# Squared-ReLU attention and a gated MLP on one core: loading and turning q and k of batches 2 to 7 in another way

## The chip, the core and the metric

The kernel runs on one core of a Trainium2 chip. The metric is the time of one execution on the device in microseconds (us). The core has five engines that each work through their own instructions in order: TensorE (PE), VectorE (DVE), ScalarE (ACT), GpSimd (POOL) and SyncE (SP, which only issues DMAs here). PEld is the loading of weights into TensorE, which overlaps its matmuls. DMAs run on 16 DMA engines; SP, ACT and POOL issue them.

## What is computed

```python
# q, k, v: (8 batches, 12 heads, 448 positions, 64), float32
scores = scale * np.matmul(q, k.transpose(0, 1, 3, 2))
attn = np.maximum(scores, 0.0) ** 2 / S
x = (attn @ v).transpose(0, 2, 1, 3).reshape(B * S, H * D)     # (3584, 768)
h = x @ w_in                                                   # w_in  (768, 2048)
g = h * (1.0 / (1.0 + np.exp(-1.702 * h)))
out = g @ w_out                                                # w_out (2048, 768)
```

All products are made in fp16 with sums in float32; the scale and 1/S are applied later, in the gelu (L201) and on the way out.

## The kernel before, in words

**Units.** A batch has three units of four heads, so there are 24 units (unit 0 to 23; batch b has units 3b to 3b+2). For each unit the kernel needs q and k turned, with the head dimension on the partitions: `qT` and `kT`, 7 blocks of 128 columns each. A unit's scores are made block by block (`scores`, L147, 64x64 parts of the array, two PSUM banks a block); `relu` (L158 on DVE, L160 on ACT) brings them to SBUF as `at`, `square` (L85, L166) squares them, and `attn_v` (L178) multiplies by v into two banks; `xt_evac` copies these into `xb`, the transposed input of the MLP.

**q and k before.** Units 0 to 5 come in one way, the others in another. Unit 0 is loaded in float32 by SP (`load`, L96) and cast; units 1 to 5 are loaded by GpSimd with a cast to fp16 on the way (`load_cast`, L101). These six are turned by TensorE (`trans_pe`, L128), 14 matmuls with the identity a tile, each giving 64 columns of weights to one half of the array, and copied from PSUM (`trans_evac`, L76 or L80). Units 6 to 23 are loaded in float32 by SP (`load`) into `qst` and `kst`, one buffer each, cast by POOL, ACT or DVE (`cast`), and turned by a DMA transpose that SP issues (`trans_dma`, L116). The fp16 tiles have two buffers for q and two for k. v is always loaded by GpSimd with a cast (four buffers).

**The MLP.** A batch's first product is made with 16 blocks of w_in. Batch 0 makes it plainly (`m1`, L214, tile `ht`); from batch 1 on a seven-product scheme is used (`unit_product`, L194, tile `hx`), with sums prepared by DVE and with snapshots, additions and gelus by ACT and DVE. Each gelu leaves a float32 tile `gf` (five buffers, used in turn); `widen` (L204) scales it into the fp16 `ring`, on POOL or DVE, and that frees the gf tile. The second product (`pair_product`, L194, tile `ox`) takes two row blocks at a time by the same scheme; the results go to `osb` and out by SP (`store`).

**The order of the work** is written out by hand, as one list of short words that the loop `do` runs through under a manual schedule. Every engine gets its instructions in the order of the words, and so do the DMA queues of SP and POOL. The words that matter here: `Lq6`, `Lk6` are float32 loads by SP of unit 6, `jq4`, `jk4` casting loads by POOL, `V4` the same of v; `Q6:a` and `K6` casts, `Rq6` and `Rk6` DMA transposes; `tq4@4` the turning by TensorE into PSUM bank 4, `eq4` its copy to SBUF; `s4.6` scores of block 6 of unit 4, `r4.6.1` a relu, `x4.6` a square, `a4` the product with v, `e4.0` its copy; `jwa0`, `jwb0` the two halves of a quarter of w_in, `jo0.1` a quarter of w_out; `f0.4.1` a third of the plain product of block 4 of batch 0, `g0.4` its gelu, `v0.4` its widening; `u1.2.0` one of the seven products. `:a`, `:d` and `:p` choose ACT, DVE or POOL, and `@` the PSUM banks.

A wait of one instruction holds up whatever stands behind it on its engine. GpSimd's DMAs of both kinds of work stand in one queue with its widenings and casts.

Of the kernel before, what the change touches and what calls it, by code (L numbers as in the profile page):

```python
# [8 lines left out]
F32 = mybir.dt.float32  # L9
F16 = mybir.dt.float16  # L10
AF = mybir.ActivationFunctionType
ALU = mybir.AluOpType
# [3 lines left out]
def kernel(  # L16
# [31 lines left out]
    for name, bufs in (("cst", 1), ("kst", 1), ("qst", 1), ("k16", 2), ("q16", 2), ("v16", 4),  # L48
                       ("kT", 3), ("qT", 3), ("at", 15), ("xb", 2),
                       ("T1", 1), ("T2", 1), ("T4", 1), ("gf", 5),  # L50
                       ("as0", 1), ("as1", 1), ("osb", 3)):
        pool(name, bufs)
# [10 lines left out]
    gate = const("gate", [1, 64])  # L63
# [30 lines left out]
    def load(n, u):  # L94
        x = new(f"{n}st", [128, 2, S], F32)
        nc.sync.dma_start(out=x, in_=quad(n, u))  # L96
        units[u][n + "st"] = x
# [6 lines left out]
    def cast(n, e, u):  # L104
        x = units[u].pop(n + "st")
        if u == 0:
            c = new(f"{n}16", [128, 2, S], F16)
            copy(e, c, x)
        else:
            c = new(f"{n}16", [128, J, 2, D], F16)  # L110
            copy(e, c.rearrange("p j a d -> p a j d"), x.rearrange("p a (j d) -> p a j d", d=D))
        units[u][n + "16"] = c

    def trans_dma(n, u):
        t = new(f"{n}T", [128, J, 128], F16)
        nc.sync.dma_start_transpose(  # L116
            out=t[:, :, :], in_=units[u].pop(n + "16").rearrange("p j a d -> p (j a d)"))
        units[u][n + "T"] = t
# [4 lines left out]
    def trans_pe(n, p, u):  # L123
        ps = bank(p, "tr", F16)
        x = units[u].pop(n + "16")
        for j in range(J):
            for a in range(2):
                nc.tensor.matmul(  # L128
                    out=ps[64 * a:64 * a + 64, j * 128:(j + 1) * 128],
                    lhsT=x[:, a, 64 * j:64 * j + 64], rhs=ident[:, :], is_transpose=True)  # L130
        units[u][n + "ps"] = ps
# [176 lines left out]
    def store_part(e, p, m, h, i):  # L308
# [3 lines left out]
            NOUT + NOUT // 2 * (h - 2), NOUT + NOUT // 2 * (h - 1))  # L312
# [32 lines left out]
    def pair_product(e, p, m, n, h=None):  # L345
        c = (0, 1, 0, 1, 0, 0, 1)[n] if h is None else 2 + h
        if n < 2 or (n == 3 and h is not None):
            op[m, c] = bank(p, "ox")
# [4 lines left out]
        mm(op[m, c][:, k], lambda f: a[:, f, :], lambda f: w[:, f, k], HF, n in (0, 1, 3))  # L353

    def pair_snap(e, p, m, n):
        i, c = {0: (0, lo), 2: (0, hi), 4: (1, hi)}[n]
        copy(e, out_tile(m + i)[:, c], op[m, 0][:, 0:NOUT], 1.0 / SC)

    def pair_last(e, p, m, n, h=None):
        i, c = {1: (0, lo), 3: (1, hi), 5: (1, lo), 6: (0, hi)}[n]  # L360
        o = out_tile(m + i)[:, c][:, quarter(h)]
        if n == 5:
            copy(e, o, op[m, 0][:, 0:NOUT], 1.0 / SC)
        else:
            x = op[m, 1 if h is None else 2 + h][:, quarter(h)]
            nc.vector.scalar_tensor_tensor(out=o, in0=x, scalar=1.0 / SC, in1=o,  # L366
                                           op0=ALU.mult, op1=ALU.add)
# [13 lines left out]
    def sp_gate(e, p, i):  # L381
        nc.sync.dma_start(out=gate[0:1, :], in_=win[i][127:128, 0, 0:64])

    with tc.manual_schedule():
# [4 lines left out]
               "G": sp_gate,  # L389
# [3 lines left out]
        for n in "kq":  # L393
# [3 lines left out]
            two["R" + n] = lambda e, p, u, n=n: trans_dma(n, u)  # L397
# [22 lines left out]
        def zeros(e, p, n):  # L420
# [8 lines left out]
            "z9@0 z1 z1 jq1 z1 z1 jk1 V1 I Lq0 Lk0 z1 z1 z1 Q0:d tq0@1 eq0:a K0:d tk0@2 tq1@3 ek0 "  # L429
            "eq1 s0.5@4.5 jq2 r0.5.1:d r0.5.0 s0.1@6.7 jk2 s0.2@0.1 r0.2.1 r0.1.1:d jq3 s0.0@2.3 "  # L430
            "s0.3@5.4 r0.1.0 r0.2.0:d r0.3.1 r0.3.0:d s0.4@1.7 tk1@6 ek1 s1.6@0.4 s1.4@5.6 jk3 x0.2 "
            "r0.0.0 V0 r0.4.1 r0.0.1 x0.0 r0.4.0 r1.6.0 s0.6@2.7 x0.3 jwa0 s1.0@3.1 r1.6.1 r1.0.1 "
            "tq2@0 x0.5 eq2 s1.5@4.1 r1.4.1 r1.5.0:d s1.3@0.6 jwb0 r1.4.0 r1.5.1 V2 s1.1@4.5 x1.6 "
            "tk2@1 jq4 r1.3.1 jwb2 x1.4 r0.6.1 ek2 r1.1.1 x0.4 jk4 r0.6.0 jwa2 r1.1.0 r1.0.0 tq3@6 "
            "s2.3@7.1 eq3 x0.1 r1.3.0 r2.3.0 s1.2@5.2 r1.2.1 jwa1 x1.1 jwb1 x0.6 tk3@4 r2.3.1 ek3 "
            "jq5 V3 a0@3.6 r1.2.0 jk5 x1.0 jwb3 x1.2 x1.3:a s2.4@0.7 e0.1:a e0.0:a r2.4.0 s3.3@2.1 "
            "x1.5 r3.3.0:d r3.3.1 r2.4.1:d a1@4.5 e1.0:a V4 e1.1:a s2.2@6.3 r2.2.1:d jwa3 s2.5@0.2 "
            "V5 r2.2.0 x2.3 f0.2.0@1 r2.5.0 jo1.0 s2.0@7.4 r2.0.1 s2.1@5.3 r2.1.1 r2.0.0:d r2.5.1 "
            "f0.2.1 jo0.0 x2.2 f0.3.0@6 r2.1.0:d f0.3.1 x2.0 s2.6@0.4 r2.6.1 r2.6.0 s3.1@3.7 r3.1.0 "
            "s3.0@2.5 r3.1.1:d jo1.1 tq4@4 f0.1.0@0 jo0.1 r3.0.0:d eq4 x2.4 x2.6 x2.1:a f0.1.1 "  # L440
            "s3.2@3.7 x2.5:a r3.2.0 a2@2.4 tk4@3 r3.2.1:d r3.0.1 e2.0:a s3.6@7.5 e2.1 ek4 f0.3.2 "
            "r3.6.0:d x3.2 r3.6.1 f0.2.2 g0.3 g0.2 f0.1.2 g0.1 s3.5@2.4 s3.4@3.7 r3.4.0 r3.4.1 "
            "r3.5.0:d s4.4@5.6 r4.4.0:d r4.4.1 v0.2 f0.0.0@1 x3.3 f0.0.1 f0.0.2 f0.8.0@0 g0.0 "
            "s4.5@3.7 r3.5.1:d S0.1 r4.5.0 s4.6@2.5 r4.6.0:d s4.3@6.1 v0.1 f0.8.1 r4.3.0 f0.8.2 "
            "x3.6 r4.6.1 x3.5 x3.0 g0.8 v0.3 s4.2@4.3 r4.2.1 S1.1 s4.1@2.6 r4.2.0 f0.4.0@5 f0.4.1 "
            "f0.5.0@0 f0.4.2 r4.1.0 f0.5.1 x4.6:a x4.2:a G3 v0.8 f0.6.0@3 f0.6.1 r4.3.1:d r4.5.1:d "
            "x3.1 S2.1 f0.6.2 f0.5.2 x4.4 x3.4 f0.7.0@4 g0.6 tq5@2 eq5 S1.2 tk5@1 r4.1.1 g0.4 Lq6 "
            "Lk6 S2.2 ek5:a g0.5 a3@7.3 e3.1:a v0.5 s4.0@2.6 s5.2@5.1 r5.2.1 r4.0.0:d f0.11.0@0 "
            "r4.0.1:d f0.11.1 r5.2.0 f0.11.2 e3.0:a x4.0 x4.5 s5.0@3.1 g0.11 s5.4@2.6 x4.3:a r5.0.1 "
            "s5.5@5.7 f0.7.1 r5.5.1 f0.9.0@0 f0.9.1 f0.9.2 r5.0.0:d f0.7.2 r5.5.0:d s5.3@1.7 r5.4.1 "  # L450
            "x4.1 v0.6 g0.7 a4@3.5 S3.1 s5.1@6.4 r5.3.1 r5.4.0 S2.4 v0.11 v0.7 x5.0:a Q6 r5.3.0:d "
            "s5.6@7.2 S1.3 e4.0 f0.10.0@1 g0.9 S3.2 f0.10.1 v0.9:d r5.6.1 r5.1.1:d u1.2.0@3 S0.3 "
            "f0.15.0@0 x5.3:a f0.14.0@2 r5.1.0 x5.1 f0.15.1 r5.6.0:d v0.4 f0.15.2 f0.14.1 x5.2:a "
            "v0.0 g0.15 f0.10.2 x5.4 T1.1 f0.14.2 u1.3.0@4 g0.10 x5.6:a f0.13.0@6 x5.5 K6 Lk7 "
            "a5@7.0 f0.13.1 S1.4 e4.1:a S3.4 S0.2 S2.3 Lq8 f0.13.2 v0.10:d e5.0:a v0.15:d e5.1:a "
            "Rq6 T1.2 u1.0.0@1 u1.1.0@5 u1.1.1@7 S0.4 t1.0.0 Rk6 g0.14 t1.1.0 T1.3 v0.14:d b1.1.1 "
            "u1.0.2 g0.13 u1.0.1@0 u1.1.2 t1.0.2 u1.0.4 v0.13 b1.0.1 g1.1.1 v1.1.1 W1.1 g1.0.1 "
            "v1.0.1 S3.3 t1.1.2 f0.12.0@2 u1.0.3 t1.0.4 u1.1.4 t1.2.0 T1.4 b1.0.3 u1.1.3 t1.1.4 "
            "u1.3.1@6 g1.0.3 u1.0.6 K7 W2.1 b1.1.3 b1.0.6 u1.0.5 Lk8 f0.12.1 W0.1 v1.0.3 u1.1.6 "
            "u1.2.1@0 g1.0.6 W3.1 b1.1.6 g1.1.3 u1.1.5 b1.2.1 v1.0.6 g1.0.5 u1.2.2 t1.3.0 v1.1.3 "  # L460
            "u1.2.3 g1.2.1 v1.0.5:d v1.2.1 W3.2 t1.2.2 b1.3.1 f0.12.2 W0.2 W0.3 g1.1.6 u1.2.4 g0.12 "
            "p0.0@7 v0.12 t1.2.4 W1.3 Q8:a b1.2.3 v1.1.6 Lq7 u1.2.5 A0.1@0 g1.2.3 W3.3 u1.3.2 Rq8 "
            "A0.2@1 g1.2.5 W2.2 h0.0 u1.2.6 b1.2.6 g1.3.1 v1.3.1 u1.3.3 g1.1.5 W2.4 W1.2 t1.3.2 "
            "p0.1@1 V6 v1.1.5 Rk7 s6.0@2.3 r6.0.0:d A0.3 r6.0.1 v1.2.5 s6.1@0.5 r6.1.0 l0.1 u1.3.4 "
            "t1.3.4 r6.1.1 p0.2 A0.4 x6.0:a s6.2@2.3 r6.2.1 h0.2:d r6.2.0:d s6.4@0.5 r6.4.1 p0.3 "
            "W2.3 b1.3.3 Q7:a W0.4 s6.3@3.2 r6.3.1 x6.1 p0.4 W1.4 K8:p r6.4.0 r6.3.0 W3.4 h0.4 "
            "x6.3:a Rq7 Lk9 l0.3 Lq9 x6.4 u1.3.5 s6.5@5.2 s6.6@0.3 r6.6.1 g1.3.5 r6.6.0 x6.2 u1.3.6 "
            "r6.5.1:d p0.5 r6.5.0 b1.3.6 g1.2.6 s7.0@3.4 l0.5 v1.2.6 r7.0.0:d x6.5 r7.0.1 x7.0 "
            "s7.2@0.2 r7.2.1 s7.4@5.6 r7.4.1 p0.6 s7.1@7.3 s7.6@4.2 r7.4.0 V8 V7 v1.3.5 r7.1.0:d "
            "Rk8 x7.4 x6.6:a r7.1.1 a6@6.5 r7.6.0 s7.3@7.3 K9:p l0.6 Q9 r7.6.1 e6.0:a r7.3.0:d "  # L470
            "r7.3.1 s7.5@4.1 r7.5.0 Lk11 e6.1 p2.0@2 x7.6 r7.2.0 Rk9 s8.5@6.7 s8.4@3.4 x7.1 "
            "s8.2@5.0 r7.5.1 r8.5.1 r8.2.1 Rq9 p2.1@1 A2.1@1 s8.1@7.0 r8.2.0:d r8.4.1 r8.4.0 x7.2 "
            "x7.3 r8.5.0 r8.1.0:d K11:p s8.3@5.4 r8.1.1 x7.5:a r8.3.0 Rk11 r8.3.1:d x8.1:a a7@3.6 "
            "s8.0@7.0 s8.6@5.4 r8.6.0 r8.6.1 A2.2@0 h2.0:d r8.0.1:d Lq10 e7.1:a p2.2 o1 r8.0.0:d "
# [150 lines left out]
```

## Time and profile before

| | us |
|---|---|
| median of 3 runs | 362.71 (362.51 to 363.19) |
| profiled execution | 363.36 |
| its span | 361.6 |
| TensorE idle in the span | 9.8 |
| instructions in the span | 9118 |
| casting loads by GpSimd, q, k, v | 34, 224 KB each as written |
| float32 loads by SP, q and k | 38, 448 KB each |
| DMA transposes by SP | 36 |

The page of a profile shows busy times by engine, the same in 40 slices of the span, the DMA queues, the chain of waits that ended last, and groups of instructions by line and form. Other views of the same trace give stretches of time, the instructions of an engine in order, and who waited for whom. The granted TensorE clock is full throughout. A busy TensorE is not one at its peak: the ends of matmuls are modelled, so distances are read from start to start.

### The profile page before, as it was taken

How to read it: one execution, taken by the hardware profiler on the slowest of the kernel's cores; microseconds unless marked ns; L12 is line 12 of the kernel's file. 1: busy time of each engine (PE TensorE's matmuls, PEld its weight loads, DVE VectorE, ACT ScalarE, POOL GpSimd, SP SyncE). 2: the span in 40 equal slices, each digit the busy share in tenths (PEclk: the TensorE clock that was granted, in tenths of full speed). 3: DMA queues.
4: the chain of work that ended last, by engine and by line, in shares of the span. 5: the costliest groups of instructions: out<-in, count | busy, mean ns of one | idle time of the engine just before them, and what ended most of it. 6: DMA issues, size and time to landing. Idle time of an engine off the chain costs nothing.

```text
span 361.6 us, 9118 instructions
## 1 busy us (share of the span) xinstructions
PE 351.8 (97%) x3600; PEld 240.6 (67%) x3600; DVE 313.2 (87%) x578; ACT 286.0 (79%) x551; POOL 116.9 (32%) x169
## 2 busy tenths in 40 slices
PE   8799999999999999999999999999999999999995
PEld 4444458854579655896568865698579756778663
DVE  3999999999998899899988898989998898674844
ACT  3999898999988998789997799868987898427410
POOL 5735731435135424242244343254121310102000
PEclk9999999999999999999999999999999999999999
DMA  8999999679889999868699625980381101130314
GB/s 178 159 195 205 217 234 240 126 122 229 189 224 268 210 164 182 204 121 199 145 195 172 198 33 86 210 200 0 68 175 46 44 2 45 45 87 2 87 45 133
DMA packets 65388, 51.39 MB, mean 142 GB/s; under 512 B 35776, under 2 KB 62016, under 8 KB 65344
## 3 DMA queue, kind: packets, MB, share of 16 engines
q1 hardware_dynamic: 48336, 36.32, 43.0%
q0 software_dynamic: 16608, 14.09, 26.7%
q8 instruction: 28, 0.46, 0.5%
q10 hardware_dynamic: 400, 0.39, 0.3%
q14 instruction: 16, 0.13, 0.1%
HBM read 45.61 MB, written 11.01 MB: 157 GB/s over the span
## 4 chain that ended last, share of the span: by engine, by line
PE 85%; DMA 6%; DVE 4%; ACT 2%; POOL 2%; issue 1%; POOLq 0%
PE ox L194 34%; PE hx L194 32%; PE sc L147 8%; PE av L178 7%; DMA k<-in_k_dram 3%; DMA q<-in_q_dram 3%; PE ht L214 3%; PE zp L424 1%; DVE at L85 1%; DVE at L158 1%; POOL ring L204 1%; ACT at L160 1%; ACT gf L201 1%; PE tr L128 0%; DVE asum L85 0%
## 5 line engine op out<-in xcount | busy, mean ns | idle before, releaser
L160 ACT ACTIVATE at<-sc 128x448 f16<-128x448 f32 x214 | 104.9, 582 | 7.3 <-PE sc L147 7.2
L204 POOL TENSOR_SCALAR ring<-gf 128x448 f16<-128x448 f32 x94 | 58.0, 617 | 156.1 <-ACT gf L201 152.7
L194 PE MATMUL ox<-wout,ring 128*128 128x384 f16 (+1 forms) x456 | 80.3, 324 | 0.1
L194 PEld LDWEIGHTS <-ring 128*128 128x128 f16 x568 | 53.7, 98 | 35.9 <-issue 6.1
L158 DVE TENSOR_SCALAR at<-sc 128x448 f16<-128x448 f32 x122 | 72.2, 616 | 3.6 <-PE sc L147 2.7
L194 PEld LDWEIGHTS <-win 128*128 128x128 f16 x672 | 64.0, 98 | 6.6 <-issue 3.0
L85 DVE TENSOR_TENSOR at<-at 128x896 f16<-128x896 f16 x102 | 63.1, 644 | 0.3
L166 ACT ACTIVATE at<-at 128x896 f16<-128x896 f16 x66 | 62.7, 969 | 0.8 <-DVE at L158 0.5
L85 DVE TENSOR_TENSOR gf<-hx,gf 128x448 f32<-128x448 f32 x84 | 51.1, 620 | 10.8 <-PE hx L194 4.9
L201 ACT ACTIVATE gf<-gf 128x448 f32<-128x448 f32 x84 | 46.8, 573 | 15.1 <-DVE gf L85 14.9
L194 PE MATMUL hx<-xb,win 128*128 128x224 f16 x504 | 58.0, 259 | 0.0
L147 PE MATMUL sc<-qT,kT 64*64 64x448 f16 x672 | 49.7, 358 | 2.0 <-DVE kT L80 1.4
L194 PEld LDWEIGHTS <-winS 128*128 128x128 f16 x504 | 48.2, 98 | 2.7 <-issue 1.1
L76 ACT ACTIVATE gf<-hx 128x448 f32<-128x448 f32 x59 | 31.4, 542 | 13.2 <-PE hx L194 9.5
L194 PE MATMUL ox<-wT,asum 128*128 128x384 f16 (+1 forms) x232 | 41.0, 321 | 0.7 <-DVE osb L366 0.5
L194 PE MATMUL hx<-T,winS 128*128 128x224 f16 x336 | 39.7, 259 | 0.0
L178 PE MATMUL av<-at,v 64*64 64x448 f16 x672 | 37.1, 350 | 1.2 <-ACT at L160 0.7
L147 PEld LDWEIGHTS <-kT 64*64 64x64 f16 x672 | 18.0, 105 | 25.9 <-issue 18.8
L194 PEld LDWEIGHTS <-asum 128*128 128x128 f16 x232 | 21.4, 98 | 16.8 <-issue 4.4
L366 DVE SCALAR_TENSOR_TENSOR osb<-ox,osb 128x384 f32<-128x384 f32 (+1 forms) x44 | 23.3, 533 | 8.9 <-PE ox L194 6.9
L178 PEld LDWEIGHTS <-v 64*64 64x64 f16 x672 | 19.8, 106 | 14.0 <-issue 2.8
L80 POOL CAST q<-qst 128x896 f16<-128x896 f32 x13 | 13.4, 1028 | 39.6 <-DMA qT<-q 14.5
(57 smaller groups left out, 363.3 us busy)
## 6 DMA issues: line engine op xcount, KB each, us to landing
out_dram<-osb SPq DMA_DIRECT2D x52, 192.0 KB, 3.4
qst<-in_q_dram SPq DMA_DIRECT2D x19, 448.0 KB, 4.9
kst<-in_k_dram SPq DMA_DIRECT2D x19, 448.0 KB, 4.4
v<-in_v_dram POOLq DMA_DIRECT2D x24, 224.0 KB, 5.7
win<-in_moe_w_in_dram POOLq DMA_DIRECT2D x8, 384.0 KB, 12.3
wout<-in_moe_w_out_dram POOLq DMA_DIRECT2D x4, 768.0 KB, 20.6
q<-in_q_dram POOLq DMA_DIRECT2D x5, 224.0 KB, 5.3
k<-in_k_dram POOLq DMA_DIRECT2D x5, 224.0 KB, 5.9
```

What stands on the lines that cost most here:

```text
L76: nc.scalar.activation(out=o, in_=i, func=AF.Copy)
L80: eng[e].tensor_copy(out=o, in_=i)
L85: eng[e].tensor_tensor(out=o, in0=x, in1=y, op=op)
L147: nc.tensor.matmul(out=sc[a][c, 0:S], lhsT=st["kT"][r, j, c], rhs=st["qT"][r, :, c], start=True, stop=True)
L158: nc.vector.tensor_scalar(out=o, in0=i, scalar1=0.0, scalar2=None, op0=ALU.max)
L160: nc.scalar.activation(out=o, in_=i, func=AF.Relu)
L166: nc.scalar.activation(out=at, in_=at, func=AF.Square)
L178: nc.tensor.matmul(out=av[s][64 * a:64 * a + 64, 0:S], lhsT=v16[r, a, 64 * j:64 * j + 64], rhs=at[r, a, :], start=(j == 0), stop=(j == J - 1))
L194: nc.tensor.matmul(out=o, lhsT=lhs(i), rhs=rhs(i), start=start and i == 0, stop=i == n - 1, skip_group_check=True)
L201: nc.scalar.activation(out=o, in_=i, func=AF.Gelu_apprx_sigmoid, scale=1.0 / SC)
L204: eng[e].tensor_scalar(out=o, in0=i, scalar1=SC, scalar2=1.0, op0=ALU.mult, op1=ALU.mult)
L366: nc.vector.scalar_tensor_tensor(out=o, in0=x, scalar=1.0 / SC, in1=o, op0=ALU.mult, op1=ALU.add)
```

## The change

All units but unit 0 are now loaded by GpSimd's casting DMA and turned by TensorE in 64-column tiles; there are no DMA transposes, no `qst` and `kst`, and no casts but unit 0's two. q and k in fp16 have four buffers each. Unit 0 is loaded in float32 by SP into the space of `ring`, which is not yet in use, and turned by 7 matmuls of 128 columns a tile. The last row pairs may be split in other quarters. The whole list of words is in a new order, and the choices of engine and bank are new.

The counts of words, before and after: casting loads of q and k 10 and 46; float32 loads 38 and 2; turnings by TensorE 12 and 48; copies of turned tiles 10 on DVE and 2 on ACT, then 31 and 17; relus 214 on ACT and 122 on DVE, then 230 and 106; widenings 94 on POOL and 34 on DVE, then 85 and 43. The numbers of score, v, w_in and w_out products are the same.

```diff
-    for name, bufs in (("cst", 1), ("kst", 1), ("qst", 1), ("k16", 2), ("q16", 2), ("v16", 4),
+    for name, bufs in (("cst", 1), ("k16", 4), ("q16", 4), ("v16", 4),
...
-        x = new(f"{n}st", [128, 2, S], F32)
-        nc.sync.dma_start(out=x, in_=quad(n, u))
-        units[u][n + "st"] = x
+        o = "kq".index(n) * 4 * S
+        x = ring.rearrange("p f c -> p (f c)")[:, o:o + 4 * S].bitcast(F32)
+        units[u][n + "st"] = x.rearrange("p (a c) -> p a c", a=2)
+        nc.sync.dma_start(out=units[u][n + "st"], in_=quad(n, u))
...
-    def trans_dma(n, u):
-        t = new(f"{n}T", [128, J, 128], F16)
-        nc.sync.dma_start_transpose(
-            out=t[:, :, :], in_=units[u].pop(n + "16").rearrange("p j a d -> p (j a d)"))
-        units[u][n + "T"] = t
...
         for j in range(J):
+            if len(x.shape) == 2:
+                nc.tensor.matmul(out=ps[:, j * 128:(j + 1) * 128],
+                                 lhsT=x[:, j * 128:(j + 1) * 128], rhs=ident[:, :],
+                                 is_transpose=True)
+                continue
             for a in range(2):
                 nc.tensor.matmul(
...
-        if n < 2 or (n == 3 and h is not None):
+        if n < 2 or h is not None:
...
-    def sp_gate(e, p, i):
-        nc.sync.dma_start(out=gate[0:1, :], in_=win[i][127:128, 0, 0:64])
...
-        "z9@0 z1 z1 jq1 z1 z1 jk1 V1 I Lq0 Lk0 z1 z1 z1 Q0:d tq0@1 eq0:a K0:d tk0@2 tq1@3 ek0 "
-        "eq1 s0.5@4.5 jq2 r0.5.1:d r0.5.0 s0.1@6.7 jk2 s0.2@0.1 r0.2.1 r0.1.1:d jq3 s0.0@2.3 "
...
+            "Lq0 Lk0 z9@0 jq1 jk1 jq2 jk2 jq3 z1 Q0:d z1 z1 I z1 z1 z1 z1 V0 tq0@1 K0:d eq0:a jwa0 "
+            "tk0@2 jk3 ek0 tq1@3 eq1 V1 s0.4@4.5 s0.2@6.7 s0.0@0.1 r0.4.0 r0.4.1:d s0.6@2.3 jq4 "
...
+            "jq8 r3.0.1 tq4@1 r3.2.0:d r3.2.1 tk4@4 jo0.1 x2.5:a x2.3 x2.6 a2@3.6 jk7 r3.0.0 ek4 "
+            "eq4:a jq7 f0.2.0@5 e2.1 f0.2.1 e2.0:a V6 x3.4 s4.5@4.1 s3.6@6.3 r4.5.0:d r4.5.1 f0.3.2 "
+            "r3.6.0 f0.2.2 r3.6.1:d f0.0.2 g0.3 x3.0 f0.1.2 g0.2 s4.3@4.1 g0.0 s4.1@6.3 v0.2 "
+            "s3.5@0.5 r4.3.0:d r4.1.0 f0.8.0@7 v0.0 r4.1.1:d r3.5.1 f0.8.1 f0.10.0@4 g0.1 jk8 x4.1 "
+            "f0.8.2 x3.6:a S0.1 f0.10.1 f0.10.2 x3.2 r3.5.0 s4.0@6.3 v0.3:d r4.3.1 s3.1@5.2 "
+            "r4.0.0:d tk5@0 r3.1.1 tq5@1 g0.10 ek5 f0.6.0@6 r3.1.0 S2.1 f0.6.1 g0.8 x3.3 f0.6.2 "
+            "r4.0.1 f0.4.0@2 v0.8 eq5 x3.1:a f0.4.1 x3.5 jk9 f0.4.2 x4.0 s4.2@4.0 g0.4 s4.6@5.7 jq9 "
+            "a3@3.1 S2.2 g0.6 v0.4 r4.2.0:d r4.2.1 r4.6.1 v0.10 s5.5@2.6 s5.0@4.0 e3.1 r5.5.1 v0.6 "
+            "f0.7.0@7 r5.0.1:d r5.5.0 f0.7.1 v0.1 f0.7.2 e3.0:a r5.0.0:d r4.6.0 s4.4@1.6 V8 S1.1 "
+            "s5.4@0.2 s5.1@3.4 r4.4.0 x4.2 f0.12.0@5 r4.4.1 f0.15.0@1 x4.6 g0.7 f0.12.1 x4.4 r5.4.0 "
```

## The prediction

> **What bounds the kernel now.** I read the engine table first, then the chain of waits, then the windows by stage, then the waits.
>
> ```profile
> PE 351.8 (97%) x3600; PEld 240.6 (67%) x3600; DVE 313.2 (87%) x578; ACT 286.0 (79%) x551; POOL 116.9 (32%) x169
> DMA  8999999679889999868699625980381101130314
> ```
>
> TensorE is busy 97% of the span. The DMA engines are at 9 tenths in nearly every slice (9.04 us each) of the first 63 us. The windows show where TensorE is really the limit (columns: stretch, length, busy us and count of PE, PEld, DVE, ACT, POOL, clock, DMA share, GB/s):
>
> ```profile
> 0.00:54.00 54.00, 49.53 (x590) 25.95 (x590) 46.95 (x87) 45.54 (x91) 30.23 (x45) 1.00 1.15 198
> 54.00:306.00 252.00, 251.12 (x2599) 177.29 (x2599) 233.40 (x429) 221.13 (x423) 82.37 (x117) 1.00 0.71 147
> ```
>
> From 54 us, where the last product of attention and v of batch 1 (unit 5) starts, to 306 us, TensorE idles 0.9 us: what is added there lengthens the run. Before 54 us it gets through only 590 matmuls, and there the chain of waits (start, length, what) does not run through it:
>
> ```profile
> 14.55 9.83 DMA q<-in_q_dram
> ...
> 24.92 11.79 DMA k<-in_k_dram
> ...
> 37.00 0.87 POOL wout L376
> ...
> 37.95 2.26 POOL ring L204
> ...
> 40.23 0.54 ACT gf L201
> ```
>
> This is read as follows. GpSimd's DMAs complete on eight semaphores in turn, so each waits until the eighth one before it has landed: k of unit 5, the 20th, is issued at 24.92 when q of unit 4, the 12th, has landed; the 28th (w_out, 37.00) goes when the 20th has. Only then does GpSimd reach its first widening (L204), which frees one of the five gf tiles for which ScalarE's gelu (L201) waits; the waits give 1.76 us for that. GpSimd's DMA queue is thus one link from the path in the start.
>
> **Transposes on TensorE.** The order of the changed kernel has 36 more tiles (units 6 to 23, q and k) of 14 matmuls. Two neighbouring tiles of the kernel before price them:
>
> ```profile
> 39.17 0.58 PE L128 MATMUL tr<-ident,q 128*64 128x128 f16 x14
> 39.59 0.56 PE L128 MATMUL tr<-ident,k 128*64 128x128 f16 x14
> 40.07 0.38 PE L178 MATMUL av<-at,v 64*64 64x448 f16 x2
> ```
>
> From start to start one tile takes 0.42 us. A tile alone (25.81, the next matmul at 26.33) takes 0.52, so leaving the 64-column form costs 0.10. The 36 tiles stand in 19 groups: 36 x 0.42 + 19 x 0.10 = **17.0 us**, all after 54 us. Bounds: nothing, if all of it fell into array time that TensorE only seems to use, and 36 x 0.52 + 19 x 0.10 = 20.6. I take 17.0, as the rows are the same instruction.
>
> **Vector work.** 36 evacuations are added, 21 on DVE at 0.62 and 15 on ACT at 0.93; casts go, 10 on ACT at 0.94, 3 on DVE at 0.63, 23 on POOL at 1.06. The new order also moves relus (16 from DVE to ACT) and small operations. With the busy time per instruction of each group DVE gets 17.6 us more, ACT 0.4, POOL 24.4 less casting and 36 x 0.74 = 26.6 more issuing. DVE then has 331 us of a run of 380 or more, the share of before; as TensorE's own share grows by as much, I cost it at nothing. If DVE adds to TensorE's time where both are full (85 to 97 us has DVE at 11.8 and ACT at 12.0 of 12), it costs up to 5.
>
> **What goes.** 36 float loads and 36 DMA transposes leave SP, which keeps stores alone. No wait of TensorE in the list (4.7 us in all) is for a DMA transpose, so this gives nothing on the path. POOL's casts spent 14.5, 11.1 and 3.2 us waiting for a transpose or a load, and only 3.8 us of all idle time before work on gf tiles is put down to POOL. Unit 0's 7 whole transposes for 14 halves, and the regrouped last quarters (8 matmuls fewer), are within 1 us either way.
>
> The Trainium skill, DMA: Bandwidth & Descriptors, section SWDGE vs HWDGE vs iDMA, speaks against the change: GpSimd writes the descriptors of its DMAs into SBUF and DVE's two-port modes lock it out. The row says otherwise here: v's issue takes 0.77 us at 72.71, with DVE full, and 0.73 at 2.86, with DVE idle. With a DVE operation of 0.6 us before each of 36 issues the rule would make 22 us on POOL, off the path except in the start.
>
> **The start.** The new order puts more DMAs ahead of the first widening on POOL: 34 for 28, and then one more behind the second widening and two more behind the third. Into these come loads of units 6 to 9 that had been SP's and came after. The instruction order shows the same semaphores in turn, so the 34th (v of unit 6) waits for the 26th (q of unit 6), and the 37th (q of unit 9) for the 29th (k of unit 6).
> - Rate: in the kernel before, two float loads (896 KB), 14 casting loads of 224 KB and 6 w_in pieces of 384 KB, 6336 KB, landed from 0.74 to 36.71 us: 176 KB/us. The best of the first five slices (217 GB/s) has the SP loads of unit 6 in it; the fourth, 205 GB/s, is 200 KB/us.
> - Landed up to the 26th: 896 + 17 x 224 + 8 x 384 + 768 = 8544 KB: 49.3 us at the first rate, 47.7 if the rest goes at 200. Up to the 29th: 10304 KB: 59.3 or 56.5 us.
> - ScalarE: its 7th gelu (g0.4) takes the tile that POOL's first widening frees. ACT has 0.8 us more to do ahead of it than ahead of the waiting gelu of before (reached at 38.47), so arrives at 39.3. It can go at 49.3 + 0.73 (issue) + 0.62 (widening) = 50.6: 11.3 us of wait. Behind it in ACT's queue stand the relus of units 4 and 5, and TensorE waits for their banks.
> - Its 9th (g0.7) needs the widening of g0.1, which stands behind the 37th DMA and three widenings: 59.3 + 0.73 + 4 x 0.62 = 62.5. ACT comes there 4.6 us after g0.4 starts, at 55.2: 7.3 more.
> - 11.3 + 7.3 - 1.8 (the wait of before) = 16.8; at the faster rate 14.0. I take **15.5**. Bounds: 18 (at 176 with 1 us of extra queueing), and minus 4.8, since POOL's early issues no longer wait for unit 1's and 2's transposes (3.3 and 1.5 in the waits).
>
> Of the same page, section Bandwidth, the limit of HBM for one core, some 358 GB/s read: with the reads being twice the casted bytes, 16.6 MB up to the 26th would be there at 46 us, and the forecast by it 3 us less.
>
> **Sum.** The profiled execution took 363.36 us, 1.76 beside its span of 361.6; the median of the runs is 362.71, 0.65 lower, and I count from it: 362.7 + 17.0 + 15.5 = **395.2 us**. A difference under 0.2% (0.7 us) could not be told from none.
>
> **The rivals.**
> - *Only the transposes cost.* For it: the loads come early and all through one queue without SP's competition, and the rate might rise; ACT's other stalls may cover the wait. Against it: the DMA row is at 9 tenths while the queue runs almost alone. 362.7 + 17.0 = 380, from 372 (half of the tiles hidden) to 387.
> - *Faster.* The place is the array: busy time is no measure of full use, and in stretches like 85 to 97 us DVE and ACT set the pace. If all 36 tiles ran in that slack, and the start gained the 4.8 us of POOL's waits, the time is 358. It decides once fewer than 4.8 of the 17.0 us remain on the path and the start does not stall. Against it: 2599 matmuls in 252 us with 0.9 idle.
> - *Both, and DVE.* The 5 us of DVE and the 18 of the start add to 20.6: 406.
> - That the change doesn't do what it says is excluded by the order: 504 transposing matmuls more, no DMA transpose.
>
> **Chances.** Forecast (388 to 402) 0.68; only the transposes 0.22; both and DVE 0.06; faster 0.04 (0.01 of it within 0.2%). The range of 377 to 402 takes the forecast and about two thirds of the second case: 0.83. Slower 0.96, same 0.01, faster 0.03.
>
> **What would show it.** Right: among the waits of ACT's gelu for POOL's ring some 11 us around 39 to 51 and some 7 around 55 to 63; unit 5's product with v starting near 70 us instead of 54; 36 tiles of tr at 0.42 to 0.52 from start to start; TensorE still without idle time after that. Wrong: unit 5 at 54 to 58 us (then the second case), POOL's 34th DMA before 43 us, or tiles of tr whose start-to-start time is covered because the next matmul waited for DVE or ACT anyway.

## The result and the profile after

The changed kernel takes 386.69 us (median of 3 runs, 385.88 to 386.87) beside 362.71 before: ratio 1.0653, 95% interval 1.0624 to 1.0681. The profiled execution took 386.87 us with a span of 385.1, so 23.5 us of span were added. Unit 5's product with v splits them: it starts at 63.25 us instead of 54.05 (+9.2), and from there to the end it takes 321.9 us instead of 307.5 (+14.3). The prediction had 15.5 and 17.0. In the runs below that leave the start as it is (two of 14, neither tiles nor copies, no copies), unit 5 starts at 63.8, 63.1 and 62.1 us, so the first number is known to about 1 us.

The page of the kernel after gives the engines, the granted clock and the DMA engines by slices of 9.63 us:

```profile
PE 370.5 (96%) x4082; PEld 254.1 (66%) x4082; DVE 326.1 (85%) x610; ACT 287.5 (75%) x551; POOL 114.5 (30%) x173
PEclk9999779999999999999999999999999999999999
DMA  9999999108663629561168236220350110210414
```

TensorE has 482 matmuls more and is busy 18.7 us longer; the clock has a hole in the fifth and sixth slice; the DMA engines are full in the start as before, and emptier later than before (a share of 0.38 after unit 5's product, where it was 0.63), since the transposes and the float32 loads are gone. The windows of the kernel after (columns: stretch, length, busy us and count of PE, PEld, DVE, ACT, POOL, clock, DMA share, GB/s) show the two losses:

```profile
0.00:54.00 54.00, 43.25 (x495) 21.47 (x496) 37.34 (x71) 37.40 (x76) 27.78 (x44) 0.91 1.21 202
39.00:45.00 6.00, 1.50 (x32) 0.81 (x25) 1.80 (x4) 0.00 (x0) 2.29 (x3) 0.85 1.30 204
45.00:50.00 5.00, 1.58 (x9) 0.49 (x9) 0.00 (x0) 2.19 (x5) 2.63 (x5) 0.50 1.31 204
63.20:331.00 267.80, 267.80 (x3103) 190.75 (x3106) 243.11 (x457) 226.16 (x431) 73.65 (x112) 1.00 0.41 70
```

(In these rows the number behind a busy time is the count of its instructions; the clock is the third number from the right.) Up to 54 us TensorE gets through 495 matmuls instead of 590 (14 of the difference are unit 0's tiles, which need fewer). Between 39 and 50 us TensorE, VectorE and ScalarE hardly work, with the DMA engines full. From 63 to 331 us TensorE has no idle time at all. The chain of waits of the kernel after (start, length, what) says what the hole waits for:

```profile
30.91 13.78 DMA v<-in_v_dram
...
45.22 0.62 POOL q L101
...
46.33 0.12 POOL v L101
...
47.11 0.56 POOL ring L199
```

DMAs 33 and 34 of GpSimd's queue are issued at 45.22 and 46.33, about half a microsecond after the 25th and the 26th have landed (30.91 + 13.78 = 44.69, and 31.87 + 13.9 = 45.8), and only then comes the first widening (L199). ScalarE's and TensorE's timelines (start, busy, what, in brackets the idle time before and what ended it) and the list of waits show what hung on it:

```profile
47.71 1.19 ACT L196 ACTIVATE gf<-ht 128x448 f32<-128x448 f32 x2 [9.14 <-POOL ring L199]
...
53.75 0.55 ACT L196 ACTIVATE gf<-ht 128x448 f32<-128x448 f32 x1
...
56.92 0.54 ACT L196 ACTIVATE gf<-ht 128x448 f32<-128x448 f32 x1 [0.48 <-POOL ring L199]
```

```profile
48.30 1.67 PE L142 MATMUL sc<-qT,kT 64*64 64x448 f16 x8 [7.80 <-ACT gf L196]
```

```profile
ACT gf L196 <- POOL ring L199: 12.4, 8, 9.1
PE sc L142 <- ACT gf L196: 7.8, 1, 7.8
```

ScalarE's 7th and 8th gelu go at 47.71, after 9.14 us; the 9th, at 53.75, does not wait; the 10th waits 0.48. TensorE stands 7.8 us at scores of unit 5 (`s5.5@2.6` in the list of words). Their banks, 2 and 6, still hold the products that the two waiting gelus must read (`f0.4.0@2` and `f0.6.0@6`), and the scores start as the first of these gelus ends.

### The profile page after: what moved, and what is told of

Same layout as the page of the kernel before. It is cut to its first block, busy times and chain, and to the rows that moved or that the text cites. A ratio compares the mean times of both kernels' runs of the same rounds, so it can differ in the third digit from the quotient of the medians.

```text
span 385.1 us, 9956 instructions
## 1 busy us (share of the span) xinstructions
PE 370.5 (96%) x4082; PEld 254.1 (66%) x4082; DVE 326.1 (85%) x610; ACT 287.5 (75%) x551; POOL 114.5 (30%) x173
## 2 busy tenths in 40 slices
DMA packets 31950, 34.92 MB, mean 91 GB/s; under 512 B 2336, under 2 KB 28576, under 8 KB 31904
## 3 DMA queue, kind: packets, MB, share of 16 engines
HBM read 45.61 MB, written 11.01 MB: 147 GB/s over the span
## 4 chain that ended last, share of the span: by engine, by line
PE 89%; ACT 4%; DMA 4%; DVE 1%; issue 1%; POOL 0%; POOLq 0%
PE ox L189 34%; PE hx L189 30%; PE sc L142 9%; PE av L173 7%; PE tr L123 5%; DMA v<-in_v_dram 4%; ACT at L155 3%; PE ht L209 3%; PE zp L423 1%; DVE at L84 1%; ACT at L161 0%; POOL ring L199 0%; ACT gf L196 0%; DVE winS L84 0%; ACT qT L75 0%
## 5 line engine op out<-in xcount | busy, mean ns | idle before, releaser
L155 ACT ACTIVATE at<-sc 128x448 f16<-128x448 f32 x230 | 113.5, 567 | 11.9 <-PE sc L142 11.3
L199 POOL TENSOR_SCALAR ring<-gf 128x448 f16<-128x448 f32 x85 | 54.4, 640 | 158.5 <-ACT gf L196 147.8
L189 PE MATMUL ox<-wout,ring 128*128 128x384 f16 x448 | 80.2, 326 | 0.0
L153 DVE TENSOR_SCALAR at<-sc 128x448 f16<-128x448 f32 x106 | 62.9, 617 | 13.3 <-PE sc L142 12.9
L84 DVE TENSOR_TENSOR at<-at 128x896 f16<-128x896 f16 x108 | 67.2, 639 | 2.3 <-ACT at L155 1.4
L196 ACT ACTIVATE gf<-gf 128x448 f32<-128x448 f32 x84 | 47.1, 577 | 23.7 <-DVE gf L84 23.5
L142 PE MATMUL sc<-qT,kT 64*64 64x448 f16 x672 | 51.6, 365 | 9.0 <-ACT gf L196 7.8
L161 ACT ACTIVATE at<-at 128x896 f16<-128x896 f16 x60 | 57.4, 969 | 1.2 <-DVE at L153 0.9
L189 PE MATMUL hx<-xb,win 128*128 128x224 f16 x504 | 57.0, 259 | 0.0
L189 PE MATMUL ox<-wT,asum 128*128 128x384 f16 x224 | 40.6, 327 | 0.0
L101 POOL DMA_DIRECT2D v<-in_v_dram x24 | 17.3, 721 | 37.4 <-PE sc L142 31.4
```

What stands on the lines that cost most here:

```text
L84: eng[e].tensor_tensor(out=o, in0=x, in1=y, op=op)
L142: nc.tensor.matmul(out=sc[a][c, 0:S], lhsT=st["kT"][r, j, c], rhs=st["qT"][r, :, c], start=True, stop=True)
L153: nc.vector.tensor_scalar(out=o, in0=i, scalar1=0.0, scalar2=None, op0=ALU.max)
L155: nc.scalar.activation(out=o, in_=i, func=AF.Relu)
L161: nc.scalar.activation(out=at, in_=at, func=AF.Square)
L189: nc.tensor.matmul(out=o, lhsT=lhs(i), rhs=rhs(i), start=start and i == 0, stop=i == n - 1, skip_group_check=True)
```

## The experiments

There are two questions: is the start's loss due to the loads that stand ahead of the widenings in GpSimd's queue, and is the later loss TensorE's time for the tiles alone? The rivals were a late first pair of widenings or the fallen clock for the first, the copies or the new order for the second. Times are medians; each ratio is against the kernel before on the same chip.

### The start

**e1: the late loads moved behind the widenings** (kernel after, the list of words only):

```diff
- ... V5 jq6 ... jo1.0 ... jo1.1 ... jk6 ... jq8 ... jo0.1 ... jk7 ... jq7 ... V6 ... v0.2 ... jk8 ... jk9 ... jq9 ...
+ ... V5 ... jo1.0 ... jo1.1 ... jo0.1 ... v0.2 ... v0.1 jq6 V6 ... v0.11 jk6 jq8 ... v0.5 jk7 jq7 ... v1.0.1 jk8 ... v1.1.1 jk9 jq9 ...
```

> The changed kernel with the loads of q and k of units 6 to 9 and of v of unit 6 moved behind batch 0's widenings in GpSimd's queue. If the start is lost because the first widenings stand behind 34 and more DMAs, the 9.1 us wait of ACT's gelu goes, unit 5's product with v starts at 54 to 56 us instead of 63.2, and the time falls by 8 to 10 to 377 to 379. If the start is lost to something else (the rate of the loads themselves, or the new order of the attention), it stays at 384 or more.

380.98 us, ratio 1.0465 (1.0414 to 1.0517). Unit 5 starts at 52.9 us, 10.3 earlier than in the kernel after, but unit 6's product with v at 92.0 instead of 97.8: 4.5 us are given back in between. The waits of this run tell why:

```profile
ACT gf L196 <- POOL ring L199: 2.2, 4, 0.8
PE tr L123 <- DMA q<-in_q_dram: 2.8, 1, 2.8
```

ScalarE's wait is gone; TensorE now waits for unit 6's q, which I had moved too far. From unit 6's product to the end it takes 287.5 us (kernel after 287.3). The start came back as expected; the time missed its 377 to 379 by 2 us, through a new wait of the experiment's own.

**e7: the same, but unit 6's q stays where it was** (against e1; unit 6's k also goes earlier than there):

```diff
- ... v0.1 jq6 V6 ... v0.11 jk6 jq8 ...
+ ... V5 jq6 ... v0.1 V6 jk6 ... v0.11 jq8 ...
```

> As e1_late_loads (loads of units 6 to 9 moved behind batch 0's widenings), but unit 6's q keeps its early place in GpSimd's queue. If the 4.5 us that e1 gave back between unit 5 and unit 6 came from the late q of unit 6, unit 5 stays near 53 us, TensorE's wait for q after it (2.8 us in e1) goes, and the time is 376 to 378.5 us. If they came from somewhere else (the clock, the other late loads), it is 380 to 382 as e1.

377.22 us, ratio 1.0386 (1.0364 to 1.0408). Two windows of this run:

```profile
0.00:53.30 53.30, 49.44 (x576) 26.00 (x577) 46.05 (x86) 45.37 (x91) 33.26 (x50) 1.00 1.21 202
53.30:375.50 322.20, 318.29 (x3507) 227.79 (x3506) 279.52 (x525) 241.69 (x461) 81.42 (x123) 1.00 0.42 75
```

Unit 5 starts at 53.30 us, before the 54.05 of the kernel before, and the rest takes 322.2, as in the kernel after (321.9). So the whole 9.2 us of the start hang on the place of eight loads in GpSimd's queue, and none of the rest does. This run takes the loads' bytes out of the start together with their place; the next one leaves both and moves the widenings.

**e2: only the first two widenings taken from behind the queue** (given to VectorE):

```diff
- ... v0.2 ... v0.0 ...
+ ... v0.2:d ... v0.0:d ...
```

> The changed kernel with only the first two widenings (blocks 2 and 0 of batch 0) moved from GpSimd to DVE, the DMAs as they are. If the queue as a whole pins the start, the gelu of block 4 no longer waits at 39 us, but that of block 7 then waits for the widening of block 1, which still stands behind the 37th DMA at 55 us: unit 5 stays at 61 to 63 us and the time at 384 to 387. If only the first widening counts, the time falls to 377 to 379.

387.9 us, ratio 1.0664 (1.0614 to 1.0715), and unit 5 at 63.6, just above what was expected. The wait only changes its place:

```profile
ACT gf L196 <- POOL ring L199: 11.8, 7, 6.8
```

The longest wait falls from 9.1 to 6.8 us, the sum from 12.4 to 11.8. The 7th and 8th gelu go at 39.47 without a wait for the ring, with all the loads' bytes still ahead: it was the widenings' place behind the loads that held them. But the 9th waits 6.8 us until 51.04, for the widening of block 8 (50.45, behind the 35th DMA), and the 10th 2.6 us until 56.34, for one behind the 37th. The queue as a whole holds the start, not one widening. The 9th waited for block 8's widening, not for block 1's as I had expected.

**b1: six loads put into the kernel before, ahead of its first widening**, into the half of the ring not yet in use; nothing reads them:

```diff
+    def load_extra(e, p, i):
+        nc.gpsimd.dma_start(out=ring[:, 2 * i:2 * i + 2, S:2 * S], in_=quad("q", 6 + i))
...
- ... jo0.1 ...
+ ... jo0.1 jx0 jx1 jx2 jx3 jx4 jx5 ...
```

> The kernel before with six more casting loads of 224 KB, into a part of ring that is not yet in use, ahead of GpSimd's first widening. If the start is pinned by DMAs that wait for the eighth one before, the 34th waits for the 26th (9088 KB, about 50 us), the third widening ends near 53 us instead of 40.2, ACT's gelu waits some 10 to 13 us, and the time rises to 371 to 377. If only the issuing of the six counts (6 x 0.73 = 4.4 us on GpSimd), it stays below 368.

380.31 us, ratio 1.0457 (1.0405 to 1.0509); unit 5 at 70.6 instead of 54.05. The waits and, below, GpSimd's timeline of this run:

```profile
ACT gf L204 <- POOL ring L207: 16.8, 2, 16.6
```

```profile
49.48 0.70 POOL L105 DMA_DIRECT2D ring<-in_q_dram  x1 [5.54 <-DMA wout<-in_moe_w_out_dram]
53.33 0.70 POOL L105 DMA_DIRECT2D ring<-in_q_dram  x1 [3.14 <-DMA wout<-in_moe_w_out_dram]
54.10 2.50 POOL L207 TENSOR_SCALAR ring<-gf 128x448 f16<-128x448 f32 x4
```

The mechanism appears in the other kernel from loads alone, larger than I expected: the last of the six wait for w_out's pieces of 768 KB to land, as these stand eight places ahead.

**e8: TensorE kept busy in the hole** (kernel after; 220 matmuls that nobody reads, behind unit 3's product with v):

```diff
         units[u] = {"av": av}
+        if u == 3:
+            for _ in range(220):
+                nc.tensor.matmul(out=av[0][:, S:512], lhsT=ident[:, :], rhs=ident[:, 0:64],
+                                 start=True, stop=True)
```

> The kernel after, with 220 matmuls of 64 columns (some 6 to 6.5 us) into spare columns of a bank, right behind unit 3's product with v at 40.5 us, where TensorE stands idle for 7.8 us and the granted clock falls to 0.49 and 0.66 in the ten microseconds that follow. Nobody reads their result. If that fall of the clock is a part of the start's 9.2 us, the clock stays near 1.0 between 45 and 55 us and the time falls by 1 to 2.5 us, to 384 to 385.7. If TensorE isn't what the start waits for while it is slow (VectorE, ScalarE and GpSimd catching up), the clock stays up and the time stays at 386 to 387.

386.31 us, ratio 1.0648 (1.0633 to 1.0664). Two windows of this run:

```profile
45.00:50.00 5.00, 4.49 (x94) 3.40 (x94) 0.87 (x2) 2.87 (x7) 2.70 (x6) 1.00 1.31 205
50.00:55.00 5.00, 5.00 (x39) 2.19 (x40) 5.00 (x11) 4.35 (x9) 1.84 (x3) 1.00 1.29 203
```

The clock stays at 1.00 (0.50 in the kernel after from 45 to 50), unit 5 starts at 62.7 instead of 63.25, and the time is the same within the intervals. ScalarE's timeline says where the gain went:

```profile
56.45 0.55 ACT L200 ACTIVATE gf<-ht 128x448 f32<-128x448 f32 x1 [2.10 <-POOL ring L203]
```

With the full clock the 9th gelu comes 2.1 us earlier (51.66 for 53.75), but the 10th then waits 2.10 us instead of 0.48 for the widenings behind the 37th DMA. GpSimd's queue, not the slow matmuls, sets the start here. The 0.5 us at unit 5 is within the 62.1 to 63.8 us of runs with the same start.

### The tiles

**e3: two of each tile's 14 matmuls, from unit 6 on** (kernel after; the tile's first block is copied seven times):

```diff
         for j in range(J):
+            if u > 5 and j > 0:
+                continue
...
-        copy(e, t, units[u].pop(n + "ps")[:, 0:J * 128].rearrange("p (j c) -> p j c", j=J))
+        ps = units[u].pop(n + "ps")
+        if u > 5:
+            copy(e, t, ps[:, 0:128].unsqueeze(1).to_broadcast([128, J, 128]))
...
```

> The changed kernel with only the first 2 of the 14 transposing matmuls of each tile of units 6 to 23; the copy to SBUF repeats that block, so the scores of these units are not the reference's. If the transposes lie on the path, 36 x 6 x 55 ns = 11.9 us go: 374 to 376. If they run in time that TensorE only seems to use, the time stays at 384 or more.

383.6 us, ratio 1.0552 (1.05 to 1.0605). After unit 5 it takes 318.0 us, only 3.9 less, although 432 matmuls are gone, some 12 us at the 28 ns of one that b3 and b4 below give (an estimate: 7.0 us for 252). That spoke against the first term of the prediction; the next four runs take it apart.

**e4: neither tiles nor copies from unit 6 on**, the turned q and k of unit 5 used instead:

```diff
+        if u > 5:
+            units[u].pop(n + "16")
+            return
...
+        if u > 5:
+            units[u][n + "T"] = kept[n]
+            return
...
```

> The kernel after, in which units 6 to 23 are neither turned nor copied: the 36 turning tiles of TensorE and their 36 copies are left out, and scores use the turned q and k of unit 5 instead (the output is not the reference's). The loads and the order stay. If tiles and copies together are what the attention stages pay for, the stretch from unit 5's product with v to the end falls from 321.9 to 305 to 309 us (before: 307.5), and the time to 370 to 374 us; the start keeps its 9 us loss (unit 5 at 63 to 64). If the new order of the other operations costs something of its own, the stretch stays at 312 us or more and the time at 377 or more.

378.13 us, ratio 1.0408 (1.0389 to 1.0428).

**e6: all tiles, but no copies from unit 6 on** (the second of the two edits above alone):

> The kernel after with all 36 turning tiles kept on TensorE for units 6 to 23, but their 36 copies by VectorE and ScalarE left out (scores use the turned q and k of unit 5; the output is not the reference's). If TensorE alone limits the stretch after unit 5, it stays at 320 to 322 us and the time at 385 to 387. If the copies stand beside the tiles as a second limit (run e3_two_of_14 took 11.5 us of matmul time out and gained only 3.9), the stretch falls by 4 to 10 us and the time to 377 to 383.

386.58 us, ratio 1.0642 (1.062 to 1.0665). The windows after unit 5 of the kernel after, then of the runs with two of 14, with neither, and without copies:

```profile
63.20:385.10 321.90, 318.10 (x3507) 227.59 (x3506) 279.62 (x526) 241.77 (x461) 78.61 (x120) 1.00 0.38 69
```

```profile
63.80:381.80 318.00, 310.38 (x3075) 218.65 (x3074) 277.84 (x526) 240.52 (x461) 79.40 (x119) 1.00 0.38 69
```

```profile
63.10:376.00 312.90, 304.62 (x3003) 215.10 (x3002) 266.81 (x503) 229.27 (x447) 79.97 (x119) 1.00 0.38 71
```

```profile
62.10:384.00 321.90, 318.06 (x3507) 227.39 (x3506) 268.28 (x504) 230.56 (x447) 78.68 (x120) 1.00 0.38 69
```

The copies alone are worth nothing: 321.9 us with and without them, although VectorE and ScalarE lose 11 us each. With the tiles in place TensorE is the limit. Take 12 of each tile's 14 matmuls out, and its idle time grows from 3.8 us (321.90 - 318.10) to 7.6; take the other two and the copies out as well, and the stretch is 9.0 us shorter than in the kernel after, with 8.3 us idle. In both runs TensorE waits in this stretch for ScalarE and VectorE, some 3 and 4 us by the list of waits, where the kernel after has no such wait. So the other engines seem to be next in line: without the tiles they, with their order, hold TensorE up. How much of the last 5.1 us (318.0 to 312.9) is due to the copies no run shows, since e4 leaves out the rest of the tiles with them. This run is still 5.4 us longer after unit 5 than the kernel before, so an order made around the tiles does not become the old one when they go. Taking them out thus shows less than they cost, and the tiles had to be added to the old order.

**b3: the tiles' matmuls alone, in the kernel before**, two tiles' worth ahead of each product with v, nothing else touched:

```diff
         av = [bank(p, "av") for _ in range(2)]
+        for i in range(28 if u > 5 else 0):
+            a = 64 * (i % 2)
+            nc.tensor.matmul(out=av[0][a:a + 64, S:512].bitcast(F16), lhsT=ident[:, 0:64],
+                             rhs=ident[:, :], is_transpose=True)
```

> The kernel before, with its order, loads and transposes by DMA untouched, and only TensorE's share of the turning added: ahead of the product with v of each of units 6 to 23, 28 transposing matmuls of 64 columns (two tiles' worth, 18 x 0.90 = 16.2 us by the groups of the kernel after) from the identity into spare columns of the product's bank; nobody reads them and nothing is copied. If TensorE is full after unit 5, as the prediction has it, the time rises by 15 to 18 us, to 378 to 381. If the order of the kernel before leaves TensorE idle time that such tiles can use (run e4_no_turn gained only 9.0 us by taking all 36 tiles out), it rises by 8 to 12, to 371 to 375.

379.63 us, ratio 1.0459 (1.0438 to 1.0481).

**b4: the same with half of them** (14 for 28):

> The same with 14 transposing matmuls, one tile's worth, for each unit from 6 on (18 x 0.51 = 9.2 us by the groups of the kernel after). TensorE full: a rise of 8.5 to 10 us, to 371.5 to 373. Idle time that covers the first tiles: a rise of 2 to 6, under half of what the run with 28 adds.

372.09 us, ratio 1.0259 (1.024 to 1.0278). The windows after unit 5 of the kernel before, of the run with 28 and of the run with 14:

```profile
54.05:361.60 307.55, 302.25 (x3011) 214.63 (x3010) 266.15 (x492) 240.38 (x461) 86.65 (x124) 1.00 0.63 132
```

```profile
53.90:377.50 323.60, 319.19 (x3515) 226.62 (x3514) 266.36 (x492) 242.19 (x461) 85.88 (x124) 1.00 0.60 126
```

```profile
53.50:370.00 316.50, 312.21 (x3263) 219.77 (x3262) 265.92 (x492) 241.55 (x461) 87.91 (x124) 1.00 0.63 129
```

From unit 5's product (53.91 and 53.51 us) to the end of the span (377.5 and 370.1) it takes 323.6 us with 28 and 316.6 with 14, so 16.0 and 9.0 more than before (307.55), where the tiles' own start-to-start time says 16.2 and 9.2; the medians rise by 16.9 and 9.4. TensorE's time goes into the run nearly one to one, from the first tile on: its idle time in the stretch only falls from 5.3 us to 4.4 and 4.3.

### A version to beat both

**b2: two of the four w_out loads moved behind the third and fourth widening** (kernel before):

```diff
- ... jo1.1 ... jo0.1 ... v0.3 ... v0.8 ...
+ ... v0.3 jo1.1 ... v0.8 jo0.1 ...
```

> The kernel before with two of the four w_out loads moved in GpSimd's queue from ahead of the first widening to behind the third and fourth. In the kernel before ScalarE waits 2.7 us in all (longest 1.8) for the ring, because GpSimd reaches its first widening late. If that wait is on the path, the time falls by 1 to 2 us, to 360.7 to 361.7 beside 362.7. If the next thing is late by as much (VectorE, or TensorE's own work), it stays within 0.5 us. It ends above 363.5 if a moved load is late for the first product with w_out.

362.34 us beside 363.15 for the kernel before on the same chip, ratio 0.9978 (0.9964 to 0.9992): 0.8 us faster. It beats both kernels, by less than expected. ScalarE's 2.7 us of waits for the ring are gone from the list. But the profiled execution (363.28 us, one of the slower ones of its 12) does not show where the gain lies: unit 3's product with v starts 1.1 us later than in that of the kernel before (41.15 for 40.07), without the stop of 0.37 us that it has there, and ends 0.3 us later; by unit 5 both are level (53.99 and 54.05). Whether that late start belongs to this execution alone was not settled.

## Why the prediction was right and where its sizes were off

The mechanisms of the two terms were right but for two links in the start, their sizes too large: 15.5 + 17.0 predicted, 9.2 + 14.3 measured. The 386.69 us lie below the 388 to 402 of the forecast itself, among the 372 to 387 of *Only the transposes*, although both losses are there: that the wider range of 377 to 402 holds them is owed to the share of the rival that it took in.

- **The tiles (17.0).** Right. The timeline of TensorE in the kernel after has a pair of tiles as it was priced:

```profile
125.63 0.58 PE L123 MATMUL tr<-ident,k 128*64 128x128 f16 x14
126.05 0.56 PE L123 MATMUL tr<-ident,q 128*64 128x128 f16 x14
126.53 0.75 PE L189 MATMUL hx<-xb,win 128*128 128x224 f16 x6
```

From start to start, 0.90 us for two (2 x 0.42 + 0.10 = 0.94 in the prediction). All 36 tiles take 16.6 us from start to start, and b3 and b4 show that TensorE's added time goes onto the run nearly whole. The stretch grew by 14.3 only. Summed over the two timelines by kind of work, from each start to the next, scores and products with v take 2.1 us less than in the kernel before, the second product 0.6 less, the first product 0.4 more: 16.6 - 2.1 - 0.6 + 0.4 = 14.3. So the new order spares some 2.3 us of TensorE's time elsewhere, which the prediction had put at nothing. Which part of it does this was not tried.
- **Vector work (nothing).** Right: e6 took the copies out and gained nothing. VectorE's busy time rose by 12.9 us, not by 17.6. The cover looks thin: with some 12 us of TensorE's matmuls gone, e3 gained only 3.9.
- **What goes (nothing).** No run takes the DMA transposes out alone. b3 keeps them and takes 16.0 us more after unit 5, the kernel after 14.3: their leaving, the new order and all the rest of the change come to a net 1.7 us there.
- **The start (15.5).** The place and the chain were right: the 34th DMA, the first widening, ScalarE's 7th gelu, TensorE's scores. e7 gives all of it back by moving eight loads. The last link was another one: the scores waited for the banks of the gelus themselves, not of the relus behind them. Two sizes failed.
  - *Rate.* The 26th DMA landed at 45.8 us, not 49.3, and the 34th went at 46.33. The 176 KB/us were those of the kernel before, and the kernel after moves more from the start: 197, 204, 203 and 202 GB/s in its first four slices, where the kernel before has 178, 159, 195 and 205. GpSimd's early waits for unit 1's and 2's transposes (3.3 and 1.5 us), which the prediction had as a bound of its own, are gone from its first 10 us; no run takes this apart. The windows have 202 GB/s up to 54 us, 197 KB/us, and my second value, 47.7 at 200 KB/us, was the better one. The first wait is 9.14 us for 11.3.
  - *"Its 9th (g0.7) needs the widening of g0.1"* was false, and is the step that failed. The 9th gelu went at 53.75 without a wait, while GpSimd's seventh widening, g0.1's by the order of words, ended only at 59.50 (four widenings from 55.98 take 3.52 us). The gf tiles are not used strictly in turn, as I had also written of the kernel before; a tile that an earlier widening had freed was taken, and in e2 the 9th gelu starts at 51.04 just as block 8's widening ends (50.45 + 0.56). The wait for the widenings behind the 37th DMA does exist, but it is the 10th gelu's, and the 37th went at 55.20 instead of 59.3: of 7.3 us there remain 0.48 and 0.35, of the 10th and 11th gelu.
  - 9.14 + 0.83 - 1.8 = 8.2 of the measured 9.2. The last 1.0 is no more than the spread between runs with the same start; e8 gives no sign that the clock is a part of it.
- **The estimate by the skill's page.** The Trainium skill, DMA: Bandwidth & Descriptors, section Bandwidth, gives each core some 358 GB/s when both cores of an HBM domain stream, and by it the 26th DMA would land at 46 us (an estimate), nearest of all to the 45.8. But it was right by accident: the rows of 202 to 204 GB/s count fp16 as written (the profile of the kernel after has 34.92 MB moved, of which 11.01 are the output, but 45.61 MB read from HBM), so the casting DMAs read about 406 GB/s of float32 (an estimate: twice 203). The measurement decides.
- **GpSimd's descriptors and VectorE.** The lockout of the same page, section SWDGE vs HWDGE vs iDMA, did not show in the issues: those at 43.78, 45.22 and 46.33, with VectorE idle, took 0.70 us each, those at 54.00, 55.20 and 59.56, with VectorE at work, 0.75, 0.70 and 0.75. Whether VectorE's operations there were in a two-port mode the traces do not say. The widenings did grow longer, from 0.6 us at 47.11 to 0.9 at 55.98, with VectorE at work; the reason was not sought.
- **The rivals.** *Only the transposes* is what e7 measures: 377.2 us with an undisturbed start (380 predicted). *Faster* fell with b4: half of the tiles already cost 9.0 us. *Both, and DVE* fell with e6.

## What to carry to other kernels

A load that becomes a DMA of a computing engine takes a place in that engine's instruction stream: count what is queued behind it, and move it behind the work that others wait for (here eight loads, 9.5 us). Work added to an engine with no idle time costs nearly its whole start-to-start time; to learn that price add it to the old order, since taking it out of the new one only shows what is next in line (9.0 us against 16.0). Before adding up waits for buffers, find out which release each allocation really takes. A stop that goes on one engine can come back as a wait on another (e8: 2.1 us earlier, then a wait of 2.10 instead of 0.48).

## What the runs showed of the hardware

- TensorE had no matmul from 40.5 to 48.30 us. In windows of 1 us the granted clock was 1.00 from 42 to 43 us, 0.58 from 43 to 44, 0.50 from 44 to 53, 0.80 from 53 to 54 and 1.00 after that. The Trainium skill, TensorE: Matmul & The Clock Gate, Part 1, has the clock at half after an idle window of about 3.4 us. The rows agree on the half; here the fall came some 2.7 us after the last matmul (an estimate from the 0.58, with the matmul's end as modelled). With the array kept busy the clock stayed at 1.00, and the time was the same: here half a clock was free, as GpSimd's queue set the pace.
- A short DMA waits for a long one eight places ahead in GpSimd's queue: 5.54 and 3.14 us for 768 KB pieces in b1, where the 33rd and 34th stand behind the 25th and 26th.
- Blocks of 28 and 14 transposing matmuls of 64 columns cost 0.89 and 0.50 us a block when added to a full TensorE (16.0 / 18 and 9.0 / 18), as their start-to-start times had it.
